# Two weight loads exchange buffers, query copies move to GpSimd, and 48 increments are put ahead of VectorE's work

## The chip, the cores and the metric

The kernel runs on one core of a Trainium2 chip. Times are device microseconds of that core. Below, PE is TensorE's matmul, PEld its weight load, DVE is VectorE, ACT ScalarE, POOL GpSimd and SP SyncE, whose queue issues nearly all loads. Time before: 378.86 us, the median of 3 runs (378.81 to 379.39).

## The reference

One decode step for two sequences (B = 2): a layer norm, grouped-query attention against a key and value cache (16 query heads, 8 key heads, 4096 positions, head size 256), and a bilinear gated feed-forward block whose result, through a silu, scales the attention's output.

```python
xn = _layernorm(x)                                  # x: 2 x 1 x 448
q = (xn @ wq).reshape(B, Sq, Hq, Dh).transpose(0, 2, 1, 3)
k = jnp.repeat(k_cache, rep, axis=1)                # rep = 2
v = jnp.repeat(v_cache, rep, axis=1)
p = _softmax(jnp.einsum("bhqd,bhkd->bhqk", q, k) * Dh ** -0.5)
s = jnp.einsum("bhqk,bhkd->bhqd", p, v).transpose(0, 2, 1, 3).reshape(B, Sq, Hq * Dh) @ wo
g = _silu(((xn @ w_gate) * (xn @ w_up)) @ w_down)   # F = 1792
return x + s * g
```

All data are float32. The caches are 4 MB for keys and 4 MB for values in each of the 16 pairs of key head and sequence.

## The kernel before

The work is 16 steps, one for each pair i of key head and sequence. Step i multiplies queries with the key block `k{i}` (`scores`), takes a softmax (`peak`, `peak_of_all`, `exponential`, `turned`), and multiplies with the value block `v{i}` (`values`). Ahead of the steps come the layer norm, the two halves of the query projection (`query(0)`, `query(1)`) and the feed-forward block (`ffn_in` with the gate's and the up weights, `ffn_out` with w_down).

Large data pass through three buffers of SBUF: the two of `ring` (16384 columns each) and the one of `slot` (13440 columns). A load is planned with its names, its buffer and its source (lines 281 to 291), and `issue` puts the planned loads on SP in that order. Before the change:

- `wq0`, the first part of w_q: ring buffer 1, its first 7168 columns
- `wg wu`, the gate's and the up weights (`wgu`): slot
- `wd wq1`, w_down with the second part of w_q (`wdq`): ring buffer 0
- `k0`, the first key block (`first`): ring buffer 1, behind `wq0`
- `v0 k1` (source `vk`): the next ring buffer, which is 0; `v1 k2`: ring buffer 1; `wo`: slot; `v2 k3`: ring buffer 0, and so on by turns

The first four are issued at once. A later load first waits until everything that reads the buffer it overwrites has been done, and since SP works in order, the loads behind it wait too.

The program is recorded first. Each operation is noted with what it reads and writes (`Recorder`, `Flow.record`), `settle` works out which earlier operations it has to wait for, and `issue` writes the instructions of each engine in the recorded order. So nearly all instructions carry one line in the profile, L220. PE's order is: `query(0)`, `ffn_in`, `ffn_out`, `query(1)`, `scores(0)`, and then a loop that PE alone runs as a hardware loop, seven turns of two steps. In a turn PE's waits are gates: semaphores that the awaited operation raises and PE lowers again (L172).

Within a turn, `values(i)` is followed by `scores(i + 1)`. Its queries are first copied from `qT` into one of two small buffers `qc`, so that PE's loop finds them in the same place in each turn:

```python
q = copy()
ACT.copy(q, query_of(i + 1))
s = scores(i + 1, q, two())
```

At the start VectorE waits for x and does the layer norm; GpSimd makes constants and has no work afterwards. `LEAD` is the number of increments of a semaphore named `lead` that VectorE's program begins with; nothing waits for that semaphore. Before the change it is 0.

Of the kernel before, what the change touches and what calls it, by code (L numbers as in the profile page):

```python
# [21 lines left out]
PART = 14 * (D + 512)  # L22
EPS = 1e-5
WQ = 14 * 512
LEAD = 0


class Flow:
# [115 lines left out]
    def issue(self):  # L144
        nc = self.nc
        lead = nc.alloc_semaphore("lead")
        for _ in range(LEAD):
            nc.vector.sem_inc(lead)
# [75 lines left out]
def gated_decode_block(nc, x, first, vk, last0, last1, wq0, wdq, wo, wgu, out):  # L224
    flow = Flow(nc)
    PE, DVE, ACT, POOL, SP = [getattr(flow, e) for e in ("PE", "DVE", "ACT", "POOL", "SP")]
# [15 lines left out]
    ring = Ring("ring", [128, 2 * ROW], 2, 512)  # L242
    slot = Ring("slot", [128, PART], 1, 512)
# [7 lines left out]
    def two():  # L251
        pairs.append(pairs.pop(0))
        return pairs[-1]

    def bank(name=None):
        return banks[name] if name else two()[:, 0]
# [6 lines left out]
    def issue(n=1):  # L263
        for names, place, src, cuts in todo[:n]:
            t = place()
            width = ROW if not names[0].startswith("w") else src.shape[1] // len(names)
            for i, name in enumerate(names):
                loaded[name] = t[:, i * width:(i + 1) * width]
            if names == ["wd", "wq1"]:
                loaded["wd"], loaded["wq1"] = t[:, :14 * D], t[:, 14 * D:]  # L270
            for lo, hi in zip(cuts, cuts[1:]):
                SP.dma_start(t[:, lo:hi], src[:, lo:hi])
        del todo[:n]

    def plan(names, place, src, cuts=None):
        todo.append((names.split(), place, src, cuts or [0, src.shape[1]]))
# [2 lines left out]
        return ring.bufs[1][:, WQ:]  # L279

    plan("wq0", lambda: ring.bufs[1], wq0)
    plan("wg wu", slot, wgu)
    plan("wd wq1", lambda: ring.bufs[0], wdq)
    plan("k0", behind, first)
    for i in range(LAST):
        plan(f"v{i} k{i + 1}", ring, vk[i])
# [138 lines left out]
    def query_of(i):  # L425
        g, b = divmod(i, B)
        return qT[g // 4][:, b, g % 4].rearrange("p d r j -> p d (r j)")

    def scores(i, q, s, halves=(0, 1)):
        k = loaded[f"k{i}"].rearrange("p (h d c n) -> p h d c n", h=2, d=2, c=NT)  # L430
        for h in halves:
            for d in range(2):
                for c in range(NT):
                    PE.matmul(s[W * c:W * (c + 1), h, :], q[:, d], k[:, h, d, c, :], start=d == 0, stop=d == 1)
        return s
# [31 lines left out]
    def softmax(i, s):  # L467
        m = peak(s)
        return turned(exponential(i, s, m, peak_of_all(m)), work["pT"]())
# [4 lines left out]
    def total(add):  # L474
        sm = bank("sm")
        PE.matmul(sm[:, :B], add.rearrange("p a r j -> p (a r j)"), su, start=True, stop=True)
        DVE.reciprocal(over, sm[:, :B])

    def values(i, pT, o):

        for e in range(KB):
            h, t, at = e // 8, e % NT, e % 8 * 2 * W
            PE.matmul(o[W * t:W * (t + 1), :], pT[:, h, at:at + 2 * W:2],
                             loaded[f"v{i}"][:, e * 512:(e + 1) * 512], start=e < NT, stop=e >= KB - NT)

    def combine(ob):
        cb = bank("cb")
        src = ob.rearrange("p s (e d c k) -> p s e d c k", e=2, d=2, c=NT)
        for e in range(2):
            for c in range(NT):  # L490
                PE.matmul(cb[W * c:W * (c + 1), :B * 64], add_blocks[:, e].rearrange("p r j -> p (r j)"),
                                 src[:, :, e, :, c, :], start=e == 0, stop=e == 1)
        return cb[:, :B * 64]

    def turn(oT, g, cb):
        DVE.transpose(oT[:, g].rearrange("p d r (b j) -> p b d r j", b=B),
                      cb.rearrange("p (b d r j) -> p b d r j", b=B, d=2, r=REP))
# [26 lines left out]
    for first in range(0, LAST, B):  # L524
        flow.turn = first
        issue(2)
        if first == 0:
            flow.turn = None
            issue()
            flow.turn = first  # L530
        for i in range(first, first + B):
            p = softmax(i, s)
            o = bank("o")
            values(i, p, o)
            DVE.tensor_copy(ob[:, i % B], o)
            q = copy()
            ACT.copy(q, query_of(i + 1))
            s = scores(i + 1, q, two())
        total(add_head)
        cb = combine(ob)  # L540
        t = work["h"]()[:, :B * 64]
        DVE.tensor_tensor(t.rearrange("p (s k) -> p s k", s=B), cb.rearrange("p (s k) -> p s k", s=B),
                          over[:, :, None].to_broadcast([128, B, 64]), op=OP.mult)
        turn(oT, first // B, t)
# [82 lines left out]
```

## Time and profile before

| What | Value |
|---|---|
| median of 3 runs | 378.86 us |
| the profiled execution's own time | 379.15 us |
| its span, first to last instruction | 377.8 us |
| HBM read | 158.54 MB |
| mean rate over the span | 420 GB/s |
| busy: PE, DVE, ACT, POOL | 189.9, 75.5, 28.6, 2.4 us |
| mean granted TensorE clock | 0.761 |

The profile is of one execution. A row of the timeline gives start, duration, engine, line, operation, output<-inputs, shape, a count where like ones are merged, and in brackets the idle time before it with what ended it. "PEq L172" there is PE's sequencer at a gate. A row of the waits gives who waited for whom: total, times, longest. A row of windows gives a stretch, its length, the busy time of PE, PEld, DVE, ACT and POOL with their counts, the granted clock, the share of time in which the 16 DMA engines were busy, and GB/s. A row of the DMA issues ends with the time from issue to landing; a row of the DMA queues has packets, MB and the share of 16 engines' time.

### The profile page before, as it was taken

How to read it: one execution, taken by the hardware profiler on the slowest of the kernel's cores; microseconds unless marked ns; L12 is line 12 of the kernel's file. 1: busy time of each engine (PE TensorE's matmuls, PEld its weight loads, DVE VectorE, ACT ScalarE, POOL GpSimd, SP SyncE). 2: the span in 40 equal slices, each digit the busy share in tenths (PEclk: the TensorE clock that was granted, in tenths of full speed). 3: DMA queues.
4: the chain of work that ended last, by engine and by line, in shares of the span. 5: the costliest groups of instructions: out<-in, count | busy, mean ns of one | idle time of the engine just before them, and what ended most of it. 6: DMA issues, size and time to landing. Idle time of an engine off the chain costs nothing. (4 is left out here: it accounts for less than half of the span.)

```text
span 377.8 us, 3298 instructions
## 1 busy us (share of the span) xinstructions
PE 189.9 (50%) x1474; PEld 57.6 (15%) x1474; DVE 75.5 (20%) x124; ACT 28.6 (8%) x58; POOL 2.4 (1%) x14
## 2 busy tenths in 40 slices
PE   0827391090730373727282719190909092808776
PEld 0201120020210020202020202020202020202223
DVE  2101013003040021312113211312130304030430
ACT  1101011001010001010101010101010101010120
POOL 0100000000000000000000000000000000000000
PEclk9968598577785585959687968776867766776999
DMA  8999979999999999899999999999999999989995
GB/s 340 474 437 410 412 281 430 402 397 437 433 476 444 444 430 423 382 438 444 444 437 444 444 437 444 430 409 395 444 444 444 437 444 444 437 389 406 435 421 233
DMA packets 3898, 158.68 MB, mean 420 GB/s; under 512 B 562, under 2 KB 692, under 8 KB 820
## 3 DMA queue, kind: packets, MB, share of 16 engines
q1 hardware_dynamic: 3888, 158.59, 97.5%
q8 instruction: 4, 0.07, 0.1%
q14 instruction: 2, 0.02, 0.0%
q10 hardware_dynamic: 4, 0.00, 0.0%
HBM read 158.54 MB, written 0.06 MB: 420 GB/s over the span
## 5 line engine op out<-in xcount | busy, mean ns | idle before, releaser
L220 PE MATMUL o<-ring,pT 128*32 128x512 f32 x480 | 82.4, 848 | 118.2 <-PEq L172 118.2
L220 PE MATMUL s<-ring,qc 128*32 128x512 f32 x448 | 50.7, 592 | 0.0
L220 PEld LDWEIGHTS o<-ring,pT 128*32 128x32 f32 x480 | 20.8, 149 | 167.2 <-issue 167.2
L220 DVE COPY ob<-o 128x512 f32<-128x512 f32 x14 | 9.7, 691 | 159.9 <-PE o L220 159.9
L220 ACT ACTIVATE p<-s,m 128x1024 f32<-128x1024 f32 x16 | 17.8, 1114 | 289.7 <-DVE m L220 289.7
L220 DVE TENSOR_REDUCE m<-s 128x1 f32<-128x1024 f32 x16 | 19.3, 1204 | 21.8 <-PE s L220 21.8
L220 DVE STREAM_TRANSPOSE pT<-p 128x1024 f32<-128x1024 f32 x15 | 18.7, 1245 | 19.1 <-ACT p L220 19.1
L220 PEld LDWEIGHTS s<-ring,qc 128*32 128x32 f32 x448 | 15.1, 110 | 33.2 <-issue 33.2
L220 PE MATMUL sm<-ident,m 128*1 128x128 f32 x16 | 4.4, 276 | 25.6 <-PEq L172 23.7
L220 DVE TENSOR_REDUCE mx<-sm 1x128 f32<-1x512 f32 x16 | 10.9, 679 | 8.1 <-PE sm L220 8.1
L220 PE MATMUL s<-slot,xnT 128*32 128x448 f32 x48 | 7.2, 748 | 7.4 <-DMA slot<-wgu 7.4
L220 PE MATMUL s<-ring,hT 128*32 128x448 f32 x28 | 5.5, 903 | 8.4 <-DMA ring<-wdq 8.4
L220 PE MATMUL sm<-one,mx 1*128 1x1 f32 x16 | 3.2, 201 | 12.9 <-PEq L172 12.1
L220 PE MATMUL s<-ring,xnT 128*32 128x512 f32 x48 | 8.1, 825 | 0.0
L220 PE MATMUL s<-ring,qT 128*32 128x512 f32 x64 | 7.5, 597 | 0.0
L220 PEld LDWEIGHTS sm<-ident,m 128*1 128x1 f32 x16 | 1.3, 79 | 35.1 <-issue 32.9
L220 DVE RECIPROCAL over<-sm 128x2 f32<-128x2 f32 x8 | 1.4, 171 | 23.9 <-PE sm L220 23.9
L220 PE MATMUL s<-ident,pT 2*128 2x2 f32 x4 | 0.6, 246 | 10.7 <-DVE pT L220 10.7
L220 PE MATMUL cb<-ob,add_blocks 128*32 128x128 f32 x128 | 5.2, 279 | 0.6 <-ACT ob L220 0.6
L220 PE MATMUL wide<-slot,oT 128*32 128x448 f32 x48 | 4.9, 539 | 0.0
L220 PEld LDWEIGHTS sm<-one,mx 1*128 1x128 f32 x16 | 2.3, 142 | 16.6 <-issue 15.7
L220 PE MATMUL s<-ring,slot 128*32 128x512 f32 x32 | 3.6, 596 | 1.1 <-DMA ring<-last 1.1
(65 smaller groups left out, 63.7 us busy)
## 6 DMA issues: line engine op xcount, KB each, us to landing
ring<-last SPq DMA_DIRECT2D x2, 4096.0 KB, 27.1
ring<-wdq SPq DMA_DIRECT2D x1, 6720.0 KB, 42.4
slot<-wgu SPq DMA_DIRECT2D x1, 6272.0 KB, 25.4
slot<-wo SPq DMA_DIRECT2D x1, 5376.0 KB, 51.1
ring<-first SPq DMA_DIRECT2D x1, 4096.0 KB, 51.4
ring<-wq SPq DMA_DIRECT2D x1, 3584.0 KB, 11.0
ring<-last SPq DMA_DIRECT2D x1, 3072.0 KB, 21.9
ring<-last SPq DMA_DIRECT2D x1, 1120.0 KB, 24.4
```

The source lines that it names most:

```text
L220: self.flow.record(self.engine, lambda: method(out, *args, **kw), writes, reads, name == "dma_start")
```

## The change

Three edits. The gate's and up weights are loaded into ring buffer 0, and w_down with w_q's second part into the slot. The fourteen copies of queries in the loop are done by GpSimd instead of ScalarE. VectorE's program begins with 48 increments of the semaphore `lead`.

```diff
-LEAD = 0
+LEAD = 48
...
     plan("wq0", lambda: ring.bufs[1], wq0)
-    plan("wg wu", slot, wgu)
-    plan("wd wq1", lambda: ring.bufs[0], wdq)
+    plan("wg wu", lambda: ring.bufs[0], wgu)
+    plan("wd wq1", slot, wdq)
     plan("k0", behind, first)
...
             q = copy()
-            ACT.copy(q, query_of(i + 1))
+            POOL.tensor_copy(q, query_of(i + 1))
             s = scores(i + 1, q, two())
```

## The prediction

> **What bounds the kernel now.** I read the page first, down to its chain of work that ended last.
>
> ```profile
> span 377.8 us, 3298 instructions
> PE 189.9 (50%) x1474; PEld 57.6 (15%) x1474; DVE 75.5 (20%) x124; ACT 28.6 (8%) x58; POOL 2.4 (1%) x14
> ...
> GB/s 340 474 437 410 412 281 430 402 397 437 433 476 444 444 430 423 382 438 444 444 437 444 444 437 444 430 409 395 444 444 444 437 444 444 437 389 406 435 421 233
> ...
> q1 hardware_dynamic: 3888, 158.59, 97.5%
> ...
> DMA ring<-last 6%; PE s L220 2%; PE o L220 1%; ACT ob L220 0%; PE cb L220 0%; DVE gate L220 0%
> ```
>
> No engine is busy for more than half of the span, while the one queue of loads keeps its sixteen DMA engines busy for 97.5% of it, and the chain ends on the loads of the last keys and values. The kernel is a stream of loads; only what makes that stream start later or pause can move the time. In the row by slices one slice falls far out between the start and the end: the sixth, 281 GB/s from 47.2 to 56.7 us. I cut it out with windows, beside a long undisturbed stretch.
>
> ```profile
> 51.60:55.40 3.80, 3.80 (x36) 0.95 (x31) 0.90 (x2) 0.84 (x1) 0.00 (x0) 1.00 0.02 9
> 107.00:340.00 233.00, 110.73 (x818) 33.77 (x818) 50.62 (x75) 16.05 (x36) 0.00 (x0) 0.73 1.00 434
> ```
>
> The last two columns are DMA share and GB/s: 0.02 and 9 in the 3.8 us, against 1.00 and 434 in the 233 us. The queue is empty there. Why it is empty stands in the waits of the SP queue, the issues with their times to landing, and the timeline.
>
> ```profile
> SPq L220 <- PE s L220: 55.0, 2, 51.7
> ```
> ```profile
> ring<-wdq SPq DMA_DIRECT2D x1, 6720.0 KB, 42.4
> slot<-wgu SPq DMA_DIRECT2D x1, 6272.0 KB, 25.4
> ring<-first SPq DMA_DIRECT2D x1, 4096.0 KB, 51.4
> ```
> ```profile
> 1.17 0.43 SPq L220 DMA_DIRECT2D slot<-wgu  x1
> 1.65 0.42 SPq L220 DMA_DIRECT2D ring<-wdq  x1
> 2.11 0.59 SPq L220 DMA_DIRECT2D ring<-first  x1
> ...
> 26.59 4.71 PE L220 MATMUL s<-slot,xnT 128*32 128x448 f32 x24 [7.36 <-DMA slot<-wgu]
> ...
> 34.74 0.97 PE L220 MATMUL s<-slot,oT 128*64 128x448 f32 x4
> ...
> 53.32 1.08 PE L220 MATMUL s<-ring,oT 128*64 128x512 f32 x4
> ...
> 54.33 3.64 PE L220 MATMUL s<-ring,qT 128*32 128x512 f32 x32
> ...
> 54.44 3.92 SPq L220 DMA_DIRECT2D ring<-vk  x2
> 58.40 0.44 SPq L220 DMA_DIRECT2D slot<-wo  x1
> ```
>
> SP stands 51.7 us before the first `vk` load, until 54.44. That load overwrites ring buffer 0, whose last reader is `query(1)`, the second part of w_q: its last four matmuls run from 53.32 to 54.40. The key block issued before it (`first`) landed at 2.11 + 51.4 = 53.5, so for about 4 us nothing was queued.
>
> **The change part by part.**
>
> Exchange of buffers. The gate's weights (`wgu`) now occupy ring buffer 0, and `wdq` the slot. Ring buffer 0 is then last read by `ffn_in`, whose final matmuls end at 34.74 + 0.97 = 35.71. The first `vk` load can be issued then, some 18.7 us earlier, behind `wdq` and `first`, which are still moving. It stays third in SP's order, with nothing put ahead of it. The second `vk` load waits as before for the first scores (54.33 + 3.64; it is the later of the x2 row, issued at 54.44 + 3.92 - 0.33 = 58.03); `wo` behind it now waits for `query(1)`, done at 54.40, so for nothing new. No byte is added. Next come the prices: the first and second `vk` loads, each alone, and the step of the steady stream from the PE starts that wait for a landing.
>
> ```profile
> ring<-vk SPq DMA_DIRECT2D x1, 21.8
> ```
> ```profile
> ring<-vk SPq DMA_DIRECT2D x1, 38.8
> ```
> ```profile
> 128.91 6.20 PE L220 MATMUL o<-ring,pT 128*32 128x512 f32 x32 [19.17 <-PEq L172]
> ...
> 148.21 5.09 PE L220 MATMUL o<-ring,pT 128*32 128x512 f32 x32 [6.87 <-PEq L172]
> ...
> 341.64 5.66 PE L220 MATMUL o<-ring,pT 128*32 128x512 f32 x32 [8.14 <-PEq L172]
> ```
>
> From 128.91 to 341.64 there are eleven loads of 8 MB: 212.73 / 11 = 19.34 us each, back to back. The first `vk` load took 21.8 from issue, so 2.4 us is start-up of an empty queue. Before: landings at 54.44 + 21.8 = 76.2 and 58.03 + 38.8 = 96.8. After: behind the key block, 53.5 + 19.34 = 72.85, then 92.2. The first landing gains 3.4 us, the second 4.65. They differ because before, the second took 20.6 us after the first, not 19.34. What took the 1.25 us shows among the DMA queues, in windows at 41 to 44 and 82 to 85 us (the same row in both) and at 354 to 358 us.
>
> ```profile
> q8 instruction: 1, 0.02, 2.0%
> ```
> ```profile
> q8 instruction: 1, 0.02, 1.4%
> ```
>
> Each is one 16 KB refill of instructions: 2.0% of sixteen engines over 3 us is 0.96 us of one DMA engine. That engine lags behind the other fifteen, and a load has landed only when the slowest is in. The refill at 42 us made one lag (the 0.02 of the empty window is 1.2 us of a single engine); the pause let it catch up; the refill at 83 us made one lag again. Without a pause the first lag stays. If the second falls on another engine they lie side by side and 4.65 us holds; on the same engine they add, 1.25 is lost, and 3.4 is left. The third refill is the row that decides.
>
> ```profile
> 327.36 0.33 SPq L220 DMA_DIRECT2D ring<-last  x1
> ```
> ```profile
> 330.80 0.33 SPq L220 DMA_DIRECT2D ring<-last  x1
> ```
> ```profile
> ring<-last SPq DMA_DIRECT2D x1, 4096.0 KB, 23.8
> ```
> ```profile
> ring<-last SPq DMA_DIRECT2D x1, 4096.0 KB, 30.3
> ```
>
> These two half loads land at 351.2 and 361.1, 9.9 apart, with the refill at 355 us between; half a step is 9.67. It added 0.3 and not 1.25, so it fell on another engine than the lagging one. I take side by side, 4.65, with 3.4 as the other end. The Trainium skill ("Runtime: NRT & Kernel Launch", Instruction fetch mechanics) calls the crossing of a 16 KiB block one tail-bump, mostly hidden. By that rule no lag would exist before or after, and every landing would come 3.4 us earlier; the trace, with 20.6 us where a step is 19.34, does not agree.
>
> Everything later waits on landings, so it moves along. SP's later issues must stay ahead of the drain.
>
> ```profile
> 137.93 0.62 PE L220 MATMUL s<-ring,qc 128*32 128x512 f32 x4
> 138.60 0.33 SPq L220 DMA_DIRECT2D ring<-vk  x1
> ...
> 148.21 1.08 PE L220 MATMUL o<-ring,pT 128*32 128x512 f32 x4 [6.87 <-PEq L172]
> ```
>
> This load is issued when the scores end, 9.6 us before the one in flight lands; less 2.4 of start-up, 7.2 us of margin a step. The new second load, issued at 58.03, faces a drain at 72.85.
>
> Query copies to GpSimd. Fourteen ACT copies go and fourteen GpSimd copies come. The nearest rows:
>
> ```profile
> L220 ACT COPY qc<-qT 128x64 f32<-128x64 f32 x14 | 3.3, 233 | 0.0
> ```
> ```profile
> L220 POOL COPY add_blocks<-rows 128x64 f32<-128x64 f32 x1 | 0.2, 234 | 0.0
> ```
>
> The same shape costs 233 and 234 ns. ACT's copy stands behind the exponential; GpSimd's, with nothing queued behind it in the loop, waits only for the scores two steps before those it serves, whose buffer it overwrites, so it can run more than a step ahead of need. The scores on PE wait for it, and all of PE's later work behind them. Cost 0, covered by that step; and ACT's 233 ns are no gain, since ACT is idle 92% of the span.
>
> The 48 increments. VectorE's first work waits for x; a sequencer operation is bounded by a place where PE passes one.
>
> ```profile
> 7.26 0.61 DVE L220 TENSOR_REDUCE st<-p 2x1 f32<-2x448 f32 x1 [7.26 <-DMA p<-x]
> ...
> 58.04 1.22 DVE L220 TENSOR_REDUCE m<-s 128x1 f32<-128x1024 f32 x1 [2.65 <-PE s L220]
> ...
> 59.38 0.08 PEld L220 LDWEIGHTS sm<-ident,m 128*1 128x1 f32 x1 [2.32 <-issue]
> ```
>
> The reduction ends at 59.26 and PE, past its gate, starts at 59.38: at most 0.12 us, so 48 cost at most 5.8 us, inside 7.26. If that cover were gone, another 7.36 us lies before `ffn_in` (its wait at 26.59), and 53.5 - 2.4 - 35.7 = 15.4 us before the new issue would be late. Cost 0. They also lengthen VectorE's program by 48 instructions, as ACT's loses 14, so refills move; the small ones hold one engine 0.3 us (0.6% of sixteen over 3 us):
>
> ```profile
> q14 instruction: 1, 0.01, 0.6%
> ```
>
> By the 1.25 us of a 0.96 us refill that is 0 to 0.4 us, either way; I take 0.
>
> The sum, against the profiled execution's 379.15 us: 379.15 - 4.65 = 374.5. That execution lies 0.29 above the median of 378.86, so the forecast is 378.86 - 4.65 = 374.2.
>
> **The rivals.**
>
> Refills add up on one engine: the gain is 3.4, 375.5 us. For it: one queue (q8) carries all of them. Against it: the 0.3 us at 355.
>
> The gain comes back in part: a later load is issued too late and a pause reappears. For it: each step has only 7.2 us of margin. Against it: that margin is set by landings and moves along. With 1 to 4 us returned, 375.5 to 378.
>
> The load isn't released earlier, because something else holds SP until 54.4. Against it: the waits name PE alone. 378.9 us.
>
> Slower: GpSimd's copies come late. One copy is wanted a step, and each can start over a step ahead, so GpSimd becomes the bound when a copy with its waits takes longer than a step, 19.34 us; it eats the whole gain from 19.34 + 4.65 / 14 = 19.7 us, and at 20.0 us the kernel would be 14 x 0.66 - 4.65 = 4.6 slower, 383.5. For it: no GpSimd work runs in the loop before, so no row shows what its waits cost there. Against it: 234 ns a copy.
>
> **How the numbers follow.** Side by side 0.63; added on one engine 0.20; partly returned 0.09; no effect 0.05; slower 0.03. The likeliest gives 374.2, with 373.5 to 374.9 its own range (0.4 for small refills, 0.3 for the runs). Reaching over the second case, 375.5, and its spread: 373.4 to 375.9 holds 0.85: the first two cases and a little of the third. What this kernel's runs can tell from no change is 0.2%, 0.8 us: faster 0.92, same 0.05, slower 0.03.
>
> **What would show it.** Right: SP issues the first `vk` load near 35.7; the window after 51.6 moves some 434 GB/s; values(0) starts near 72.9 and the second near 92.2; the two half loads land near 346.5 and 356.5, and what follows them is as long as before. Same engine: the second step again 20.6. GpSimd shows 14 copies of 0.2 to 0.3 us with none waited for. Wrong would be an empty stretch of the queue anywhere later, VectorE starting after 7.3, or `wdq` landing later than 44.0 because the new load shares the engines with it.

## The result and the profile after

| | before | after |
|---|---|---|
| median | 378.84 us (4 runs, 378.13 to 379.39) | 374.68 us (4 runs, 374.30 to 375.43) |
| ratio | | 0.9894, 95% interval 0.9871 to 0.9917 |
| the profiled execution: time, span | 379.15, 377.8 us | 374.30, 372.7 us |

The changed kernel is 4.2 us faster by the medians; 374.2 was forecast. The page of the kernel after, the same lines as of before:

```profile
span 372.7 us, 3346 instructions
...
GB/s 339 466 424 410 429 433 450 443 445 396 425 459 436 450 443 436 429 394 450 436 450 443 436 429 394 450 436 450 443 436 429 394 450 436 450 397 443 421 414 233
...
q1 hardware_dynamic: 3888, 158.59, 98.6%
...
DMA ring<-last 6%; PE o L220 2%; PE s L220 1%; DVE gate L220 0%
```

The sixth slice reads 433 GB/s where it read 281. Other slices differ too, since shorter slices cut the loads at other places, but between the first and the last none is below 394. The bytes are the same and the chain still ends on the last loads, so what went is the pause. The wait of the SP queue, its issues, and the starts of PE that wait for a landing, of the kernel after:

```profile
SPq L220 <- PE s L220: 54.5, 2, 33.1
```
```profile
7.07 0.61 DVE L220 TENSOR_REDUCE st<-p 2x1 f32<-2x448 f32 x1 [7.07 <-DMA p<-x]
...
34.88 0.97 PE L220 MATMUL s<-ring,oT 128*64 128x448 f32 x4
35.89 22.13 SPq L220 DMA_DIRECT2D ring<-vk  x2
...
72.77 5.03 PE L220 MATMUL o<-ring,pT 128*32 128x512 f32 x32 [12.38 <-PEq L172]
```
```profile
92.18 5.56 PE L220 MATMUL o<-ring,pT 128*32 128x512 f32 x32 [8.19 <-PEq L172]
```

SP now stands 33.1 us instead of 51.7 and issues the first `vk` load at 35.89, as `ffn_in` ends (34.88 + 0.97). The same starts in the kernel before:

```profile
76.33 5.19 PE L220 MATMUL o<-ring,pT 128*32 128x512 f32 x32 [15.60 <-PEq L172]
96.94 5.13 PE L220 MATMUL o<-ring,pT 128*32 128x512 f32 x32 [9.23 <-PEq L172]
```

The first values start 3.56 us earlier, the second 4.76. The forecast of the landings was 72.85 and 92.2.

### The profile page after: what moved, and what is told of

It is laid out like the page before. It is cut to its first block, busy times and chain, and to the rows that moved or that the text cites. A ratio compares the mean times of both kernels' runs of the same rounds, so it can differ in the third digit from the quotient of the medians.

```text
span 372.7 us, 3346 instructions
## 1 busy us (share of the span) xinstructions
PE 188.0 (50%) x1474; PEld 57.2 (15%) x1474; DVE 75.5 (20%) x124; ACT 26.7 (7%) x44; POOL 5.6 (2%) x28
## 5 line engine op out<-in xcount | busy, mean ns | idle before, releaser
L220 PE MATMUL o<-ring,pT 128*32 128x512 f32 x480 | 81.4, 840 | 115.3 <-PEq L172 115.3
L220 DVE TENSOR_REDUCE m<-s 128x1 f32<-128x1024 f32 x16 | 19.3, 1205 | 21.9 <-PE s L220 21.9
L220 PE MATMUL s<-ring,xnT 128*32 128x448 f32 (+1 forms) x72 | 12.1, 828 | 8.3 <-DMA ring<-wgu 8.3
L220 PE MATMUL s<-slot,hT 128*32 128x448 f32 x28 | 5.4, 885 | 8.0 <-DMA slot<-wdq 8.0
L220 POOL COPY qc<-qT 128x64 f32<-128x64 f32 x14 | 3.2, 236 | 290.9 <-PE s L220 283.6
L220 PEld LDWEIGHTS s<-ring,xnT 128*32 128x32 f32 x72 | 2.6, 145 | 17.0 <-DMA ring<-wgu 9.2
L220 PE MATMUL s<-ring,oT 128*32 128x112 f32 (+2 forms) x76 | 5.1, 314 | 0.1
```

Of the source, the lines that this page charges most:

```text
L220: self.flow.record(self.engine, lambda: method(out, *args, **kw), writes, reads, name == "dma_start")
```

## The experiments

Each is told with its edit, what was expected, and what was measured. The kernel before, run again on the same chips, had medians of 378.76 to 378.83 us.

**The exchange alone.** LEAD stays 0 and the copies stay on ScalarE.

```diff
-    plan("wg wu", slot, wgu)
-    plan("wd wq1", lambda: ring.bufs[0], wdq)
+    plan("wg wu", lambda: ring.bufs[0], wgu)
+    plan("wd wq1", slot, wdq)
```

> The kernel before with the exchange of buffers alone; query copies stay on ScalarE, no increments. Theory (the pause of the load queue near 51.6 to 55.4 us is all of it): the first vk load is issued near 35.9, the second step's values start near 92, time within 0.5 us of the changed kernel, about 374.7. Rival (the instruction refills that the other two edits move out of the stream take part): at least 0.8 us above the changed kernel, 375.5 or more.

Measured 374.20 us (5 runs, 374.01 to 375.03), ratio 0.9886 (0.9867 to 0.9905).

```profile
34.60 24.14 SPq L220 DMA_DIRECT2D ring<-vk  x2
```
```profile
72.92 5.68 PE L220 MATMUL o<-ring,pT 128*32 128x512 f32 x32 [11.81 <-PEq L172]
92.37 6.19 PE L220 MATMUL o<-ring,pT 128*32 128x512 f32 x32 [7.58 <-PEq L172]
```

The issue is early and both starts are those of the whole change, within 0.2 us. The exchange brings all of the gain.

**The other two edits, each alone.**

```diff
-            ACT.copy(q, query_of(i + 1))
+            POOL.tensor_copy(q, query_of(i + 1))
```

> The kernel before with the query copies on GpSimd alone. Theory: covered, no change, 378.8 within 0.5 us, and the 8 KB instruction transfer that lay near 374 us is gone, since ScalarE's program is 14 instructions shorter. Rival (that transfer sits among the last loads and costs): 0.4 us or more faster than before. Rival (GpSimd's copies come late): slower by more than 0.8 us.

Measured 378.86 us (12 runs, 377.92 to 379.87), ratio 1.0003 (0.9990 to 1.0016): no change. The rows of the small instruction transfers, of before and then of this kernel:

```profile
q14 instruction: 2, 0.02, 0.0%
```
```profile
q14 instruction: 1, 0.01, 0.0%
```

One of two is gone, as expected, and it cost nothing that can be measured.

```diff
-LEAD = 0
+LEAD = 48
```

> The kernel before with the 48 increments alone. Theory: they end near 5.1 us, before x lands near 7.0; the 8 KB instruction transfer near 163 us moves to near 11 us and its lag is taken up by the pause; no change, 378.8 within 0.5 us. Rival (VectorE's moved refill costs or gains): off by 0.4 us or more.

Measured 379.38 us (12 runs, 378.08 to 379.88), ratio 1.0015 (1.0002 to 1.0028). That is 0.6 us above the kernel before, a little over the bound expected. The spans do not stand apart (median 377.7 us against 377.5 of the kernel before), so the reason is sought outside the span, further below.

**The pause put back, the buffers kept.** In the changed kernel `wo` is planned ahead of the `vk` loads, and issued ahead of them.

```diff
+    plan("wo", slot, wo)
     for i in range(LAST):
         plan(f"v{i} k{i + 1}", ring, vk[i])
-        if i == 1:
-            plan("wo", slot, wo)
...
-        flow.turn = first
-        issue(2)
         if first == 0:
             flow.turn = None
             issue()
-            flow.turn = first
+        flow.turn = first
+        issue(2)
```

> The changed kernel with one line moved: the load of wo (into the slot, which query(1) releases at 54.1 us) is issued ahead of the first vk load instead of third, so SP stands until 54.1 again although ring buffer 0 is free at 35.9. Same bytes, same buffers. Theory: the queue runs empty as before, from about 51.7 to 55.4; the time goes back to that of the kernel before, about 378.8 (378.2 to 379.4). Rival (the placement of the weights itself matters, not the pause): stays near 374.7.

Measured 378.62 us (12 runs, 377.41 to 379.80), ratio 1.0002 (0.9987 to 1.0017).

```profile
53.40 0.33 SPq L220 DMA_DIRECT2D slot<-wo  x1
```
```profile
44.00:76.00 32.00, 13.63 (x98) 3.71 (x98) 5.11 (x8) 2.75 (x4) 0.00 (x0) 0.71 0.95 401
```
```profile
44.00:76.00 32.00, 13.53 (x98) 3.71 (x98) 5.11 (x8) 2.88 (x5) 0.00 (x0) 0.71 0.93 392
```
```profile
44.00:76.00 32.00, 16.50 (x118) 4.53 (x122) 5.11 (x8) 2.75 (x4) 0.00 (x0) 0.72 1.04 450
```

The three windows are this kernel, the one before, and the changed one. From 44 to 76 us the queue moved 401 GB/s here against 450 with the `vk` load in front. The weights lie where the change puts them and the gain in time is gone: it hung on the pause, not on the placement. SP stood until 53.40, a little less than the 54.1 expected, since `wo` does not reach the columns that `query(1)` reads last.

**More increments: how far the cover reaches.** The changed kernel with `LEAD = 200`:

> The changed kernel with 200 increments instead of 48. At the 93 ns each that they took there, VectorE starts near 19.2 instead of 7.1 us, the layer norm and query(0) are 12.2 us later, ffn_in starts near 31 instead of 27.2, the first vk load is issued near 40, still ahead of the drain at about 51. Theory: no change, 374.7 within 0.5 us. Rival (the early chain is already close to the path): slower by about 4 us, the delay of ffn_in.

Measured 374.68 us (4 runs, 374.66 to 374.90), ratio 0.9892 (0.9870 to 0.9913).

```profile
20.18 0.61 DVE L220 TENSOR_REDUCE st<-p 2x1 f32<-2x448 f32 x1 [20.18 <-issue]
```
```profile
38.30 0.33 SPq L220 DMA_DIRECT2D ring<-vk  x1
```
```profile
72.86 6.08 PE L220 MATMUL o<-ring,pT 128*32 128x512 f32 x32 [12.98 <-PEq L172]
```

VectorE starts 13.1 us later than in the changed kernel, the load is issued only 2.4 us later because `ffn_in` finds its weights landed, and the values start at 72.86 as before: up to there 13 us of delay are free, and the rival, 4 us slower, falls. The equal time hides a later loss. Near the end one step is longer, and it holds the third 8 KB transfer of VectorE's instructions:

```profile
297.95 6.17 PE L220 MATMUL o<-ring,pT 128*32 128x512 f32 x32 [7.50 <-PEq L172]
318.17 6.30 PE L220 MATMUL o<-ring,pT 128*32 128x512 f32 x32 [6.37 <-PEq L172]
```
```profile
q14 instruction: 1, 0.01, 0.6%
```

The row of the queue is of 313 to 316 us. The step is 20.22 us, 0.9 more than 19.3, and the span of this execution is 373.4 where the changed kernel has 372.7. The time is the same only because this kernel spends some 0.3 us less outside the span, of which more below.

With `LEAD = 400`:

> The changed kernel with 400 increments. VectorE starts near 37.7 us, 30.7 later; ffn_in ends near 58.3 and the first vk load is issued then, so the queue stands empty for about 6 us. Theory: it lands 21.8 later at 80.1 and the second 20.6 after it at 100.7, where the changed kernel has 92.0: 8.7 us slower, 383.4 (382.5 to 384.5). Rival (a pause of the queue is caught up later, by ring buffers that come free early): less than half of that.

Measured 381.49 us (4 runs, 381.01 to 382.39), ratio to the kernel before 1.0065 (1.0042 to 1.0088): 6.8 us above the changed kernel. The rival falls, but the figure was 1.9 us too high.

```profile
57.50 13.41 SPq L220 DMA_DIRECT2D ring<-vk  x2
```
```profile
80.71 5.09 PE L220 MATMUL o<-ring,pT 128*32 128x512 f32 x32 [7.43 <-PEq L172]
100.04 5.66 PE L220 MATMUL o<-ring,pT 128*32 128x512 f32 x32 [8.05 <-PEq L172]
```

The issue came 0.8 us earlier than reckoned, and the second step is 19.33 us where I had put 20.6: both first refills of TensorE (66.7 and 88.4 us) now came after the pause, so, by the theory, the first `vk` load already carried one lag (80.71 is 23.2 us behind its issue, against 21.9 in the kernel before) and the second refill lay beside it. The profiled execution is 7.86 us behind the changed kernel's at the second start (100.04 less 92.18).

**The refills themselves.** The kernel before with 180 increments ahead of TensorE's program.

```diff
-LEAD = 0
+LEAD = 180
...
-            nc.vector.sem_inc(lead)
+            nc.tensor.sem_inc(lead)
```

> The kernel before with 180 increments ahead of TensorE's program instead of none on VectorE; nothing waits for them. They move its first two 16 KB instruction refills, at 42.0 and 82.9 us before, ahead of the pause near 52 us. Theory (each refill makes one DMA engine lag 1.25 us, and a pause of the queue takes the lag up): the step from the first to the second vk landing is 19.3 us instead of 20.6, and the time 1 to 1.3 us below the kernel before, about 377.6. Rival (the longer step has another cause): step still 20.6, time 378.8.

Measured 377.53 us (12 runs, 376.44 to 378.55), ratio 0.9963 (0.9948 to 0.9977).

```profile
52.18 5.43 SPq L220 DMA_DIRECT2D ring<-vk  x2
```
```profile
73.94 5.89 PE L220 MATMUL o<-ring,pT 128*32 128x512 f32 x32 [13.96 <-PEq L172]
93.25 6.47 PE L220 MATMUL o<-ring,pT 128*32 128x512 f32 x32 [7.24 <-PEq L172]
126.57 5.18 PE L220 MATMUL o<-ring,pT 128*32 128x512 f32 x32 [19.03 <-PEq L172]
```
```profile
q8 instruction: 1, 0.02, 1.8%
```

The step from the first to the second start is 19.31 us where the kernel before has 20.61 (76.33 to 96.94): with the refill moved to 51 us the lag is gone, as expected. The row of the DMA queues is a third refill, at 98.9 us, inside the stream; the next stretch, with `wo` in it, is 33.32 us long where the kernel before has 31.97 (96.94 to 128.91), so there a lag of 1.35 us comes back. What the time gained is then another thing: this kernel issued its first `vk` load 2.26 us earlier (52.18 against 54.44), and 126.57 lies 2.34 us ahead of 128.91. Why it was earlier is told in the next section. The steps show the refills; the agreement of the time with 377.6 does not.

The same 180 increments in the changed kernel, with none on VectorE:

> The changed kernel with 180 increments ahead of TensorE's program and none on VectorE. As in the kernel before with the same increments, TensorE's 16 KB refills come near 34, 51 and 99 us instead of 42 and 78, and one falls into the stream more. The first vk load is issued near 42 us, still ahead of the drain. Theory (refills fall on different DMA engines and their lags lie side by side): the steps stay 19.3 to 19.4 us and the time 374.7 within 0.5 us. Rival (lags add on one engine, or each refill holds up the whole stream): one more refill, 1.3 us slower, 376.0.

Measured 374.28 us (6 runs, 374.10 to 375.44), ratio 0.9884 (0.9863 to 0.9906).

```profile
73.05 5.63 PE L220 MATMUL o<-ring,pT 128*32 128x512 f32 x32 [12.99 <-PEq L172]
92.35 6.21 PE L220 MATMUL o<-ring,pT 128*32 128x512 f32 x32 [7.48 <-PEq L172]
124.32 5.59 PE L220 MATMUL o<-ring,pT 128*32 128x512 f32 x32 [18.08 <-PEq L172]
```

Without a pause, the refill near 96 us adds nothing: 31.97 us from 92.35 to 124.32, as in the kernel before. TensorE's refills lie side by side, as the theory has it; no view names the DMA engine of a refill, so that they use different ones is inferred from the steps.

**GpSimd under load.** The changed kernel with twelve more GpSimd copies ahead of each query copy.

```diff
+LOAD = 12
...
+    idle = sbuf([128, 512], "idle")
...
+            for _ in range(LOAD):
+                POOL.tensor_copy(idle, qT[0].rearrange("p b g d r j -> p (b g d r j)"))
             POOL.tensor_copy(q, query_of(i + 1))
```

> The changed kernel with 12 more GpSimd copies of 128x512 ahead of each query copy, whose result nothing reads: some 8 to 12 us of GpSimd work per step. Theory: a step of the load stream is 19.3 us and the copies may run ahead, so no change, 374.7 within 0.5 us. Rival (a late query copy delays the scores and through them the loads): several us slower, up to the added work beyond 7.2 us of margin in each of 14 steps.

Measured 374.54 us (4 runs, 374.32 to 375.25), ratio 0.9892 (0.9869 to 0.9915).

```profile
82.98 0.24 POOL L221 COPY qc<-qT 128x64 f32<-128x64 f32 x1 [38.68 <-PE s L221]
83.15 8.04 POOL L221 COPY idle<-qT 128x512 f32<-128x512 f32 x12
101.17 0.24 POOL L221 COPY qc<-qT 128x64 f32<-128x64 f32 x1 [9.98 <-PE s L221]
```

Eight us of extra work a step change nothing. The rows also show the limit of this test: the extra copies ran before the query copy's own wait ended, and 9.98 us of idle time were left, so no query copy was late here. That a late one costs wasn't tried.

**What the 48 increments cost.** The changed kernel again, and the exchange with one of the other edits each, on one chip.

> The changed kernel once more, beside its parts on one chip: 374.3 to 374.9, as the yardstick for the next two.

> Exchange of buffers and the 48 increments; copies on ScalarE. Theory (the increments are free): within 0.3 us of the changed kernel and of the exchange alone (374.2). Rival (the VectorE refill that they move from near 160 to near 11 us costs): 0.4 us or more above the exchange alone, with or without the GpSimd copies.

> Exchange of buffers and the GpSimd copies; no increments. Theory: within 0.3 us of the changed kernel and of the exchange alone. Rival (the ScalarE refill near the end, which goes away, costs): 0.4 us or more below the exchange alone, about 373.8.

Measured 374.62 (6 runs, 374.33 to 375.13), 374.52 (6, 374.46 to 375.16) and 374.28 us (6, 374.08 to 374.78); ratios 0.9885, 0.9890 and 0.9881, each give or take 0.002. The rival of the last of the three, 373.8, falls: no run of it was below 374.08. The rival of the second, 0.4 or more, cannot be told from the theory by time alone (374.52 against 374.20). But each run also gives its span, and the time less the span separates the kernels without overlap:

| kernels | time less span, us |
|---|---|
| 48 increments on VectorE: changed (10 runs), alone (12), `wo` first (12), GpSimd load (4), with the exchange (6) | 1.60 to 1.75 |
| none on VectorE: before (57 runs), exchange alone (5), GpSimd alone (12), both (6) | 1.26 to 1.40 |
| 200 or 400 on VectorE (4 each), 180 on TensorE (12 and 6) | 1.26 to 1.45 |

So just 48 add some 0.3 us, outside the first and last instruction, and longer programs do not. That fits an end of VectorE's program that needs one block more, which 200 and 400 place elsewhere; the views that were read show nothing of it outside the span, so this cause is argued and not shown.

## Why the prediction was right

- The pause and its cause held within 0.2 us: first issue 35.89 (35.7 forecast), starts at 72.77 and 92.18 (landings at 72.85 and 92.2). The two half loads near the end landed at 346.2 and 355.8, 0.3 and 0.7 us ahead of the forecast. The exchange alone gives the time, and a pause put back takes it away.
- The step for the refills held: "side by side, 4.65" came out as 4.76 at the second start. The kernels with moved refills show both halves of it: one refill after a pause lengthens a step by about 1.3 us, and a further one of TensorE, where another engine lags already, by nothing. A third one of VectorE did lengthen a step, by 0.9 us with 200 increments; the changed kernel has only one. The Trainium skill ("Runtime: NRT & Kernel Launch", Instruction fetch mechanics) calls such crossings mostly hidden; in this stream of loads the first one after a pause was not, with a step of 20.61 us in place of 19.31.
- The copies on GpSimd at 0: held. The kernel after has

```profile
L220 POOL COPY qc<-qT 128x64 f32<-128x64 f32 x14 | 3.2, 236 | 290.9 <-PE s L220 283.6 <-DVE qT L220 7.3
```

  236 ns each against 233 on ScalarE, waiting 290.9 us in all and with nobody waiting for it.
- The 48 increments at 0: the term that was mis-sized. Inside the span they were covered, VectorE starting at 7.07; the cover even reaches 13 us, as the 200 show. Outside it they cost 0.3 us. With 374.2 + 0.3 the forecast is within 0.2 of the median.
- The forecast took the 4.65 from one profiled execution, and the pause is not equally long in all. It ends with `query(1)`, the last reader of the buffer, which follows `ffn_out`. Rows of `ffn_out`, with the windows from 44 to 50 us behind them: the kernel before, then the same with the GpSimd copies.

```profile
44.08 5.52 PE L220 MATMUL s<-ring,hT 128*32 128x448 f32 x28 [8.36 <-DMA ring<-wdq]
43.83 4.67 PE L220 MATMUL s<-ring,hT 128*32 128x448 f32 x28 [9.04 <-DMA ring<-wdq]
```
```profile
44.00:50.00 6.00, 5.52 (x28) 1.36 (x28) 0.35 (x1) 0.00 (x0) 0.00 (x0) 0.60 0.99 426
44.00:50.00 6.00, 5.18 (x44) 1.42 (x44) 0.62 (x1) 0.23 (x1) 0.00 (x0) 0.76 1.00 431
```

  The granted clock of TensorE was 0.60 and 0.76, the first `vk` load was issued at 54.44 and 53.34, and the spans are 377.8 and 376.7 us: the 1.1 us of the issue are those of the span. With 180 increments on TensorE the clock there was 1.00 and `ffn_out` took 3.20 us, so `query(1)` ended at 52.14 (51.06 + 1.08) and the span was 375.9.

```profile
44.15 3.20 PE L220 MATMUL s<-ring,hT 128*32 128x448 f32 x28 [1.50 <-DVE hT L220]
```
```profile
51.06 1.08 PE L220 MATMUL s<-ring,oT 128*64 128x512 f32 x4
```

  By these three executions, TensorE's clock in this stretch reaches the time through the pause; in the changed kernel the load is issued long before. The spans of the kernel before run from 376.3 to 378.9 us (57 runs), those of the changed one from 372.7 to 373.8 (10 runs): the pause was probably much of the scatter too, which these ranges and the three executions suggest and no run isolates.
- That the time came out within 0.5 us is in part luck. In the two profiled executions the span fell by 5.1 us and not by 4.65: 4.76 by the second start, 5.02 by the last (341.64 to 336.62), for which no run gives a reason. Against that stand the 0.3 us of the increments, and that the 4.65 was taken off a median that lies 0.29 below the execution from which it was worked out.

The best times belong to the exchange without the increments: 374.20 alone and 374.28 with the GpSimd copies, against 374.68 and 374.62 for the whole change. The ranges of the runs overlap, so the times alone do not settle it; the 0.3 us outside the span is what speaks for leaving the increments out.

## What to carry to other kernels

In a kernel bound by one stream of loads, look for the slice in which the rate falls and ask which buffer the next load in the queue waits for; the load that is wanted first should take over the buffer that is read out first. Price a pause by the landings on both sides of it, and look at the second landing too: here a lag that the pause had hidden came to light there. Judge small edits by the time less the span as well as by the time.

## What the runs showed of the hardware

By the steps, refills of TensorE's instructions (16 KB) seem to fall on different DMA engines, those of VectorE (8 KB) on one; no view names the engine, so both are inferred. The kernel with 400 increments has three of the latter by 36 us, and its loads land later each time, though nothing else in the queue differs; rows of its issues and then of the exchange alone, which has none that early:

```profile
slot<-wdq SPq DMA_DIRECT2D x1, 6720.0 KB, 43.3
ring<-wgu SPq DMA_DIRECT2D x1, 6272.0 KB, 27.0
ring<-first SPq DMA_DIRECT2D x1, 4096.0 KB, 52.7
ring<-wq SPq DMA_DIRECT2D x1, 3584.0 KB, 11.7
```
```profile
slot<-wdq SPq DMA_DIRECT2D x1, 6720.0 KB, 42.2
ring<-wgu SPq DMA_DIRECT2D x1, 6272.0 KB, 25.4
ring<-first SPq DMA_DIRECT2D x1, 4096.0 KB, 51.4
ring<-wq SPq DMA_DIRECT2D x1, 3584.0 KB, 11.0
```

After one refill `wq` lands 0.7 us later, after two `wgu` 1.6. The `wdq` row of the second kernel carries TensorE's first refill, which the first kernel has only at 66.7 us, so three small ones cost 1.1 more than one large one. Lags of VectorE's refills thus seem to add up, which the longer step with 200 increments fits; it is the case that the prediction's first rival had in mind. It did not decide here, because the changed kernel has only one.

An increment took 93 ns on VectorE (the last of 48 stands at 5.15 us; 200 end by 20.18, at most 97 ns each) and about 0.15 us on TensorE, whose first matmul started at 28.28 us behind 180.
